# The chunk stores of the last head: from GpSimd's queue to SyncE's

## The chip, the cores and the metric

The kernel runs on one core of one Trainium2 chip. The metric is device microseconds of that core for one execution, the median of several executions. A run of a program on one core carries the state "fast" unless it lies over 1.5% above the fastest of the same kernel.

Engine names: PE is TensorE, DVE VectorE, ACT ScalarE, POOL GpSimd, SP SyncE. A "DMA engine" is one of the 16 that move bytes for this core; it is another thing than the engine that *issues* a transfer.

## The reference

Attention for one query per head, with its gradients: 64 heads (2 x 32), 8192 keys of 128 numbers, bf16.

```python
def _fwd_reference(q, k, v):
    scale = q.shape[-1] ** -0.5
    scores = jnp.einsum("bhqd,bhkd->bhqk", q, k) * scale
    p = _softmax(scores, axis=-1)
    return jnp.einsum("bhqk,bhkd->bhqd", p, v)

def reference(q, k, v, grad_out):          # shortened
    _out, _vjp = jax.vjp(_fwd_reference, q, k, v)
    return (_out, *_vjp(grad_out))          # out, dq, dk, dv
```

k and v are read once and dk and dv written once, 134 MB each: 537 MB in all, 2 MB for one head and one tensor.

## The kernel before

Every head has a tile of k and a tile of v, 128 partitions x 64 x 128 numbers (2 MB, 16 KB a partition). SyncE issues the loads, GpSimd the stores. VectorE writes dv and dk into the same tiles, in four chunks of 16 x 128 numbers a partition, and the tile is stored when its last chunk is made. Only the last head is stored chunk by chunk (4 KB a partition, 512 KB a chunk).

```python
SPREAD = range(5, 64, 9)              # heads 5, 14, 23, 32, 41, 50, 59
...
    load_eng = nc.sync
    store_eng = nc.gpsimd
    pin = tc.keep_in_program_order
...
    def by_rows(eng, dst, src, rows):
        p = 0
        for m in rows:
            pin(eng.dma_start(out=dst[p : p + m], in_=src[p : p + m], max_dma_last_dim=NT * D))
            p += m
...
    def outer(i, w, c, ends):         # one chunk of dv (w = 1) or dk (w = 0) of head i
        ...                           # VectorE writes the chunk into h.tile[w]
        if c + 1 in ends:
            at = ends.index(c + 1)
            b0, b1 = (ends[at - 1] if at else 0) * CH, (c + 1) * CH
            dst = (dv_v if w else dk_v)[i]
            if w == 0 and i in SPREAD:
                by_rows(store_eng, dst, h.tile[w], (P - 2, 2))
            else:
                pin(store_eng.dma_start(out=dst[:, b0:b1, :], in_=h.tile[w][:, b0:b1, :]))
...
    whole = [NCH]                     # NCH = 4
    last = list(range(1, NCH + 1))
...
            outer(x[0], 1, x[1], last if x[0] == BH - 1 else whole)
...
            outer(x[0], 0, x[1], last if x[0] == BH - 1 else whole)
```

The dk of the seven heads in SPREAD goes out as two stores, of 126 and of 2 rows (the *split stores*). At the very end SyncE stores two small tiles, out and dq (16 KB each).

## Time and profile before

| | before |
|---|---|
| time, median of 3 runs at the outset | 1289.55 us (1287.81 to 1290.55) |
| span of the profiled execution | 1290.8 us |
| busy: PE, ACT, DVE | 87%, 76%, 73% |
| DMA | 9 tenths or more in 39 of 40 slices |

The page of the kernel before, its DMA lines: the busy share in tenths in 40 slices of the span, what they moved, the two queues (q0 is that of GpSimd's stores, q1 that of SyncE), and the issue group of the chunk stores with the median time from issue to landing.

```profile
DMA  9999999999999999999999999999999999999994
GB/s 390 423 427 428 427 427 426 428 427 427 427 427 428 428 426 425 412 429 426 428 426 427 427 426 428 428 426 424 426 427 428 426 421 424 427 429 426 421 383 185
...
q0 software_dynamic: 20784, 268.45, 49.4%
q1 hardware_dynamic: 19020, 268.51, 48.8%
...
out_dram<-kvt POOLq DMA_DIRECT2D x8, 512.0 KB, 22.2
```

About 427 GB/s from the second slice to the last but two: the bytes bound this kernel. Only the tail is not full. Here it is in windows of 10 us (the kernel before; after the busy times come PE's granted clock, the DMA share and GB/s):

```profile
core 0: us, PE busy (x) PEld busy (x) DVE busy (x) ACT busy (x) POOL busy (x), PEclk, DMA share, GB/s
1240.00:1250.00 10.00, 7.72 (x103) 4.84 (x101) 8.50 (x24) 4.16 (x5) 0.86 (x2) 0.93 0.87 347
1250.00:1260.00 10.00, 4.64 (x19) 1.82 (x18) 9.82 (x16) 0.00 (x0) 1.79 (x4) 0.50 0.88 366
1260.00:1270.00 10.00, 0.90 (x3) 0.63 (x3) 1.19 (x5) 0.00 (x0) 1.06 (x2) 0.50 0.66 272
1270.00:1280.00 10.00, 0.00 (x0) 0.00 (x0) 0.00 (x0) 0.00 (x0) 1.06 (x2) 0.50 0.54 220
1280.00:1290.00 10.00, 0.00 (x0) 0.00 (x0) 0.00 (x0) 0.00 (x0) 0.00 (x0) 0.50 0.18 71
```

From 1262 us on nothing computes, and a third to four fifths of the DMA capacity lies idle. Why? The timeline of GpSimd, the kernel before, has the last whole store and then the eight chunks; in brackets the idle time before each and what ended it:

```profile
start us, us, engine line op out<-in xcount [idle before <-releaser]
1246.36 0.53 POOL L411 DMA_DIRECT2D out_dram<-kvt  x1 [10.33 <-DVE ld L253]
1249.67 0.53 POOL L411 DMA_DIRECT2D out_dram<-kvt  x1 [2.77 <-DVE dS_pad L325]
1251.06 0.53 POOL L411 DMA_DIRECT2D out_dram<-kvt  x1 [0.86 <-DVE dqT L379]
1254.56 0.53 POOL L411 DMA_DIRECT2D out_dram<-kvt  x1 [2.97 <-DVE sel L362]
1259.42 0.53 POOL L411 DMA_DIRECT2D out_dram<-kvt  x1 [4.33 <-DVE kvt L394]
1264.27 0.53 POOL L411 DMA_DIRECT2D out_dram<-kvt  x1 [4.31 <-issue]
1269.18 0.53 POOL L411 DMA_DIRECT2D out_dram<-kvt  x1 [4.39 <-DMA out_dram<-kvt]
1274.13 0.53 POOL L411 DMA_DIRECT2D out_dram<-kvt  x1 [4.42 <-DMA out_dram<-kvt]
1278.99 0.53 POOL L411 DMA_DIRECT2D out_dram<-kvt  x1 [4.32 <-DMA out_dram<-kvt]
```

VectorE has made the last chunk by about 1259.3; GpSimd issues its store at 1278.99. It looks like a store queue that is fed too late.

The trace's packet records tell another story. They carry no name of a DMA engine, but one DMA engine works packet after packet with next to no gap, so its row of packets can be followed back from the last packet. For the kernel before (start us, ns, queue, bytes; the records of 4 bytes are the signals that a share of a store has landed):

```
1278.079   9 q0 4        end of the laggard's share of the last 2 MB store
1278.085 159 q0 4096     first packet of chunk 1
1278.240 159 q0 4096
...                      64 packets of 4 KB, 155 ns from start to start
1287.910 159 q0 4096     last packet of chunk 8
1288.065   9 q0 4
```

This one DMA engine, the laggard, has no gap from 1248.79 to 1288.07. Its shares of six 2 MB stores (eight packets of 16 KB, 607 ns from start to start) end at 1253.64, 1258.51, 1263.37, 1268.27, 1273.22 and 1278.08, and each of GpSimd's last six issues follows such an end by about 0.9 us. GpSimd waits *for the laggard*, with eight stores outstanding; the laggard never waits for GpSimd.

### The profile page before, as it was taken

Reading aid. Unit: us, or ns where it says so; the run is one execution under the profiler, and the core shown is the slowest. Engines: PE = TensorE matmul, PEld = TensorE weight load, DVE = VectorE, ACT = ScalarE, POOL = GpSimd, SP = SyncE. Lnnn points to the kernel's source line nnn. Section 1 sums busy time; section 2 is a strip of 40 time slices with the busy share of each in tenths; the row PEclk is TensorE's granted clock in tenths of the full one; section 3 lists DMA queues with packets and bytes.
Section 4 is the critical chain, followed back from the end, with each engine's and each line's share of the span. In section 5 each row is a group of like instructions: output and inputs, shape, how many; then the busy total and the mean of one; then the engine's idle time right before and its main releaser. Section 6 shows DMA issues by size and latency. Waiting matters only on the chain.

```text
span 1290.8 us, 42577 instructions
## 1 busy us (share of the span) xinstructions
PE 1126.7 (87%) x19268; PEld 856.4 (66%) x19268; DVE 936.1 (73%) x2122; ACT 975.1 (76%) x641; POOL 79.3 (6%) x150
## 2 busy tenths in 40 slices
PE   6999999988998988989888889899898888988870
PEld 5777777666676766766666667677666666766650
DVE  2888888777787777767667777677677776777780
ACT  6888888777787777777778777778687777877740
POOL 0000000000000000000000000000000000000000
PEclk9999999999999999989999998899899999999985
DMA  9999999999999999999999999999999999999994
GB/s 390 423 427 428 427 427 426 428 427 427 427 427 428 428 426 425 412 429 426 428 426 427 427 426 428 428 426 424 426 427 428 426 421 424 427 429 426 421 383 185
DMA packets 39985, 539.67 MB, mean 418 GB/s; under 512 B 5116, under 2 KB 5116, under 8 KB 6396
## 3 DMA queue, kind: packets, MB, share of 16 engines
q0 software_dynamic: 20784, 268.45, 49.4%
q1 hardware_dynamic: 19020, 268.51, 48.8%
q8 instruction: 150, 2.46, 0.7%
q14 instruction: 31, 0.25, 0.0%
HBM read 268.47 MB, written 268.47 MB: 416 GB/s over the span
## 4 chain that ended last, share of the span: by engine, by line
DMA 37%; another core or an unknown queue 27%; PE 20%; DVE 7%; issue 5%; ACT 1%; SPq 1%; POOL 0%; POOLq 0%; ACTq 0%
DMA kvt<-in_v_dram 17%; DMA kvt<-in_k_dram 13%; PE tp L184 9%; DMA out_dram<-kvt 6%; PE acc L339 5%; DVE kvt L394 4%; PE dpw L195 3%; PE sw L195 2%; DVE sel L362 1%; ACT ev L186 1%; SPq L98 1%; PE dpw L282 1%; DMA qd_nat<-in_q_dram 1%; DVE sel L356 0%
## 5 line engine op out<-in xcount | busy, mean ns | idle before, releaser
L186 ACT COPY ev<-tp 128x2048 bf16<-128x2048 bf16 x512 | 954.3, 1865 | 269.2 <-PE tp L184 257.6
L184 PE MATMUL tp<-ident_bf,kvt 128*128 128x128 bf16 x8192 | 556.0, 222 | 99.2 <-DMA kvt<-in_v_dram 75.4
L394 DVE TENSOR_TENSOR kvt<-qb,pair 128x2048 bf16<-128x2048 bf16 x512 | 621.4, 1214 | 0.3
L184 PEld LDWEIGHTS <-kvt 128*128 128x128 bf16 x8192 | 486.4, 100 | 106.7 <-DMA kvt<-in_v_dram 79.1
L195 PEld LDWEIGHTS <-ev 128*128 128x128 bf16 x8192 | 243.1, 96 | 208.1 <-issue 150.5
L339 PE MATMUL acc<-kvt,dS_pad 128*64 128x512 bf16 x1024 | 167.3, 409 | 1.6 <-DVE dqT L379 1.6
L339 PE MATMUL acc<-kvt,E_pad 128*64 128x512 bf16 x1024 | 160.5, 394 | 0.0
L195 PE MATMUL dpw<-qdT,ev 128*128 128x1 bf16 x4096 | 140.8, 164 | 17.6 <-DVE qb L177 16.6
L362 DVE SCALAR_TENSOR_TENSOR sel<-acc,diag,sel 128x128 f32<-128x128 f32 x384 | 134.7, 351 | 13.6
L195 PE MATMUL sw<-qdT,ev 128*128 128x1 bf16 x4096 | 141.8, 164 | 1.1 <-ACT ev L186 1.1
L411 POOL DMA_DIRECT2D out_dram<-kvt x127 | 68.0, 535 | 1121.0 <-DVE kvt L394 950.5
L207 DVE TENSOR_REDUCE mp<-sw 128x1 f32<-128x64 f32 x64 | 14.4, 224 | 149.7 <-PE sw L195 149.7
L339 PEld LDWEIGHTS <-dS_pad 128*64 128x64 bf16 x1024 | 37.6, 111 | 25.1 <-issue 5.1
L247 DVE CAST E_pad<-E_f 128x64 bf16<-128x64 f32 x64 | 12.5, 195 | 55.5 <-ACT E_f L238 55.5
L339 PEld LDWEIGHTS <-E_pad 128*64 128x64 bf16 x1024 | 36.3, 108 | 21.1 <-issue 0.4
L253 DVE CUSTOM_DVE_ANT_0 junk<-E_f,dpw 128x64 bf16<-128x64 f32 x64 | 14.1, 221 | 48.9 <-PE dpw L195 48.9
L376 PE MATMUL acc<-ones,sel 128*128 128x1 f32 x256 | 43.4, 239 | 6.2 <-DVE sel L362 6.2
L282 PE MATMUL dpw<-ld,ones 128*128 128x1 f32 x256 | 46.3, 250 | 0.1
L356 DVE TENSOR_SCALAR sel<-acc,diag 128x128 f32<-128x128 f32 x128 | 44.1, 344 | 0.0
L376 PEld LDWEIGHTS acc<-ones,sel 128*128 128x128 f32 x256 | 39.1, 193 | 7.3 <-DVE sel L362 7.3
L177 DVE CAST qb<-dpw 128x128 bf16<-128x128 f32 x128 | 35.5, 277 | 6.0 <-PE dpw L168 6.0
L282 PEld LDWEIGHTS dpw<-ld,ones 128*128 128x128 f32 x256 | 38.2, 189 | 0.5 <-DVE ld L253 0.5
(44 smaller groups left out, 313.3 us busy)
## 6 DMA issues: line engine op xcount, KB each, us to landing
out_dram<-kvt POOLq DMA_DIRECT2D x119, 2048.0 KB, 67.1
kvt<-in_v_dram SPq DMA_DIRECT2D x64, 2048.0 KB, 20.9
kvt<-in_k_dram SPq DMA_DIRECT2D x63, 2048.0 KB, 21.1
out_dram<-kvt POOLq DMA_DIRECT2D x7, 2016.0 KB, 70.6
out_dram<-kvt POOLq DMA_DIRECT2D x8, 512.0 KB, 22.2
kvt<-in_k_dram SPq DMA_DIRECT2D x2, 512.0 KB, 4.4
kvt<-in_k_dram SPq DMA_DIRECT2D x1, 1024.0 KB, 7.0
out_dram<-kvt POOLq DMA_DIRECT2D x7, 32.0 KB, 70.6
```

Source lines behind the costliest of these rows:

```text
L177: pin(nc.vector.tensor_copy(out=h.qb[w][:], in_=h.qbp))
L184: pin(nc.tensor.transpose(tp[:, t, :], src[:, c * CH + t, :], ident_bf[:]))
L186: pin(nc.scalar.copy(out=ev[:], in_=tp[:]))
L195: nc.tensor.matmul(dst[:, c * CH + t : c * CH + t + 1], lhsT=ev[:, t, :], rhs=qdT[:, w, i : i + 1], start=True, stop=True,)
L207: pin(nc.vector.reduce_max(out=h.mp[:], in_=h.s, axis=AX.X))
L282: nc.tensor.matmul(out, lhsT=ones[:].to_broadcast([P, P]), rhs=col, start=True, stop=True)
L339: nc.tensor.matmul(h.acc[w][g : g + CW, :], lhsT=wts[:, n0 : n0 + CW], rhs=rows[:, n0 : n0 + QT, :].rearrange("p n d -> p (n d)"), start=( ...
L356: nc.vector.tensor_scalar(out=h.sel[:], in0=block, scalar1=diag[:, 0:1], scalar2=None, op0=ALU.mult)
L362: nc.vector.scalar_tensor_tensor(out=h.sel[:], in0=block, scalar=diag[:, b : b + 1], in1=h.sel[:], op0=ALU.mult, op1=ALU.add,)
L376: nc.tensor.matmul(h.acc[w][:, 0:1], lhsT=h.sel[:], rhs=ones[:], start=True, stop=True)
L394: nc.vector.tensor_tensor(out=h.tile[w][:, n0 : n0 + CH, :].rearrange("p n (e t) -> p n e t", t=2), in0=h.qb[w][:] .rearrange("p (e t) -> ...
L411: pin(store_eng.dma_start(out=dst[:, b0:b1, :], in_=h.tile[w][:, b0:b1, :]))
```

## The change

The intent: the eight chunk stores no longer queue behind GpSimd's waits. SyncE, which has nothing to issue after its last load, issues them as soon as the chunks are made.

```diff
             if w == 0 and i in SPREAD:
                 by_rows(store_eng, dst, h.tile[w], (P - 2, 2))
             else:
-                pin(store_eng.dma_start(out=dst[:, b0:b1, :], in_=h.tile[w][:, b0:b1, :]))
+                eng = load_eng if len(ends) > 1 else store_eng
+                pin(eng.dma_start(out=dst[:, b0:b1, :], in_=h.tile[w][:, b0:b1, :]))
```

## The prediction

> **What bounds the kernel now.** DMA: the page's 40 slices show it 9 tenths busy or more in 39, at about 427 GB/s; PE (87%), ACT (76%) and DVE (73%) are below. So only the tail, where the eight chunk stores are, can change. Windows of the tail show the DMA share falling: 0.87 (1240-1250 us), 0.88, 0.66, 0.54, 0.16 (1280-1291). Stores seem late: in the timeline GpSimd issues the eight at 1249.67, 1251.06, 1254.56, 1259.42, 1264.27, 1269.18, 1274.13 and 1278.99, although VectorE made the last chunk by about 1259.3. Waits of 4.3-4.4 us between them are for landings of earlier stores.
>
> **But those waits are not the critical path.** The trace's packet records name no DMA engine, but packets of one engine follow each other almost without a gap. Followed back from the last packet (end 1288.07), one DMA engine, the laggard, is busy without a gap from 1248.79: six groups of eight 16 KB packets (611 ns each; its shares of 2 MB stores), ending at 1253.64, 1258.51, 1263.37, 1268.27, 1273.22, 1278.08, then 64 packets of 4 KB (155 ns apart), its shares of all eight chunks. GpSimd's issues follow those group ends by about 0.9 us: it is held by the laggard's backlog (eight stores outstanding), so the laggard never starves. The DMA engines that idle (1265-1280) are those ahead of it; they finish at 1281.4-1281.8.
>
> **What the change does.**
> - Takes eight issues (0.53 us each) and waits of 4.4 us from GpSimd; adds eight issues (about 0.33 us each, as the loads') to SyncE, which has nothing to issue between 1215.5 and 1262. The chunks should go at 1249 to 1259.5: the last some 19 us earlier.
> - Bytes and shares per DMA engine stay: 128 partitions, 4 KB each. The Trainium skill ("DMA: Bandwidth & Descriptors", "Issuing engines are not separate DMA queues") says that DMAs of all issuers run on the same 16 DMA engines; here loads and stores share the 427 GB/s, which agrees. Its "Queues, rings and completion order": a DMA engine round-robins its queues by packet. So on the laggard 4 KB chunk packets will alternate with 16 KB packets of the backlog: first chunks land early, the last 2 MB store later (about 1285, not 1278), and the sum, 48 x 0.607 + 64 x 0.155 = 39.1 us from 1248.8, is the same: end about 1288.
> - The other DMA engines finish up to 15 us earlier; nothing waits for them.
> - 1288.07 to the end at 1290.8 stays. The small stores (16 KB) are now queued behind the chunks: 256 B packets of 18 ns, nothing.
>
> About 0 of the 19 us is critical.
>
> **Predicted:** 1289.3 us, 1286.0 to 1292.0 (8 in 10). Faster by over 2%: 2%; within 2%: 97%; slower: 1%.
>
> **What the profile would show.** Right: chunk issues move to SyncE and end by about 1260; GpSimd's waits of 4.4 us are gone; the DMA share rises in 1255-1265, then falls to about one engine of 16 (0.06) before 1288; the last packets end near 1288 in one gapless chain. Wrong: that chain ends before 1286, or has gaps.
>
> **What would make it wrong.** The hardware queue splits these stores otherwise, so that the laggard gets less (its 10 us of chunks, 0.8%, is the most to win); the laggard is slow because of the software queue itself; alternating two queues costs time; or the small stores wait for a chunk's landing, end last and add 1-2 us.

## The result and the profile after

| | before | after |
|---|---|---|
| median, 4 runs each | 1290.05 us (1287.81 to 1291.21) | 1287.83 us (1286.27 to 1289.27) |
| ratio | | 0.9985, 95% interval 0.9965 to 1.0004: the same |
| span of the profiled execution | 1290.8 us | 1286.9 us |
| last chunk issued | 1278.99 | by 1257.78 |
| last packet to the end of the span | 2.74 us | 2.05 us |

A ratio here is the mean time of one kernel's fast runs over that of the other's in the same rounds, so not quite the ratio of the medians quoted beside it.

The page of the kernel after, the same lines:

```profile
DMA  9999999999999999999999999999999999999995
GB/s 388 424 425 427 427 427 427 426 427 428 428 426 427 428 427 426 416 429 427 427 427 429 427 427 427 427 424 424 426 427 428 426 427 424 427 428 428 424 392 216
...
q1 hardware_dynamic: 20172, 272.70, 49.8%
q0 software_dynamic: 19632, 264.25, 48.7%
...
out_dram<-kvt SPq DMA_DIRECT2D x8, 512.0 KB, 24.0
```

4.2 MB went from q0 to q1, and a chunk takes no less time from issue to landing than before (median 24.0 us, before 22.2). The timeline of SyncE's queue after, then that of GpSimd:

```profile
start us, us, engine line op out<-in xcount [idle before <-releaser]
1245.80 11.98 SPq L412 DMA_DIRECT2D out_dram<-kvt  x8
1259.23 4.90 SPq L489 DMA_DIRECT2D out_dram<-nat  x2
```

```profile
1243.38 0.53 POOL L412 DMA_DIRECT2D out_dram<-kvt  x1 [9.19 <-DVE ld L253]
```

All eight chunks are issued within 12 us, and GpSimd's last store is issued by 1243.9. The windows of the tail after:

```profile
core 0: us, PE busy (x) PEld busy (x) DVE busy (x) ACT busy (x) POOL busy (x), PEclk, DMA share, GB/s
1240.00:1250.00 10.00, 7.76 (x68) 3.73 (x66) 9.31 (x20) 1.86 (x1) 0.53 (x1) 0.70 0.92 376
1250.00:1260.00 10.00, 3.62 (x14) 1.82 (x14) 8.03 (x17) 0.00 (x0) 0.00 (x0) 0.50 1.00 411
1260.00:1270.00 10.00, 0.00 (x0) 0.00 (x0) 0.00 (x0) 0.00 (x0) 0.00 (x0) 0.50 0.61 255
1270.00:1280.00 10.00, 0.00 (x0) 0.00 (x0) 0.00 (x0) 0.00 (x0) 0.00 (x0) 0.50 0.48 202
1280.00:1290.00 10.00, 0.00 (x0) 0.00 (x0) 0.00 (x0) 0.00 (x0) 0.00 (x0) 0.55 0.06 22
```

The DMA share is higher until 1260 and lower from there on: the DMA engines that are ahead finish sooner, and the laggard still works alone at the end (one of 16 is 0.06). Its row of packets after, in two places (in the first, the records of several DMA engines fit together with the row's end; each row that fits alternates like this):

```
1251.654 159 q1 4096     chunks and whole stores in turn
1251.809 611 q0 16384
1252.416 159 q1 4096
1252.571 611 q0 16384
...
1284.402 159 q1 4096
1284.557 159 q1 4096     last packet of chunk 8
1284.713   9 q1 4
1284.718  18 q1 256      the small stores, eight packets
...
1284.837   9 q1 4        last record
```

The two queues alternate packet by packet, without a gap: the chunks begin early and the whole stores end late. The last 2 MB store landed 12.4 us before the end of the span in before and 5.4 us in after.

**How much of the 3.9 us between the two profiled spans belongs to the change?** The lead is there before the change can act: the last load is issued at 1215.21 in before and at 1213.08 in after. Each store signals 16 landings, one for each DMA engine. I call *lag* the time from the 15th to the last of these, read at the 126-row store of head 59, which lands at 1244 to 1252 us, when no chunk is stored yet. The lag is 6.51 us in before and 3.27 us in after; the 15th landing comes at the same time in both (1242.62 and 1242.61). So the lag accounts for 3.24 us, and the last packet indeed ends 3.23 us earlier (1288.07 and 1284.85). The other 0.69 us of the 3.9 are the time from the last packet to the end, 2.74 against 2.05 us; they come up again below.

### The profile page after: what moved, and what is told of

Same layout as the page of the kernel before. It is cut to its first block, busy times and chain, and to the rows that moved or that the text cites. A ratio compares the mean times of both kernels' runs of the same rounds, so it can differ in the third digit from the quotient of the medians.

```text
span 1286.9 us, 42575 instructions
## 1 busy us (share of the span) xinstructions
PE 1131.8 (88%) x19268; PEld 860.1 (67%) x19268; DVE 935.9 (73%) x2122; ACT 975.2 (76%) x641; POOL 75.1 (6%) x142
## 4 chain that ended last, share of the span: by engine, by line
DMA 38%; PE 26%; another core or an unknown queue 19%; DVE 10%; issue 4%; ACT 1%; SPq 1%; POOL 0%; POOLq 0%; DVEq 0%; ACTq 0%
DMA kvt<-in_v_dram 29%; PE tp L184 11%; PE acc L339 6%; DVE kvt L394 6%; DMA kvt<-in_k_dram 5%; DMA out_dram<-kvt 4%; PE dpw L195 3%; PE sw L195 3%; DVE sel L362 2%; ACT ev L186 1%; PE dpw L282 1%; SPq L98 1%; DVE sel L356 1%; DMA qd_nat<-in_q_dram 1%
## 5 line engine op out<-in xcount | busy, mean ns | idle before, releaser
L412 POOL DMA_DIRECT2D out_dram<-kvt x119 | 63.7, 536 | 1087.6 <-DVE kvt L394 922.1
```

The costliest lines, as they stand in the source:

```text
L412: pin(eng.dma_start(out=dst[:, b0:b1, :], in_=h.tile[w][:, b0:b1, :]))
```

## The experiments

Two theories. **L (laggard):** the end is set by the bytes that one DMA engine still has; when the chunks are issued doesn't matter while it has a backlog. **I (issue):** the tail is bound by late issues, and what the change gained was lost again elsewhere. Times are in the table at the end of this section.

### The change again

No edit.

> The changed kernel again, in more rounds, to have its size beside the other runs. Theory L (laggard: one DMA engine has a gapless backlog that holds all its shares of the eight chunks, so the end is its bytes and not the time of issue): ratio to before 0.998 to 1.000. Theory I (issue: the DMA share falls in the tail because GpSimd issues late, so issuing 19 us earlier must pay): below 0.995.

Measured: ratio 0.9979 (0.9951 to 1.0007), 1287.2 us. An issue some 21 us earlier isn't worth 0.5%. The profiled execution had a lag of 0.3 us and a span of 1285.0 us.

### The last head whole, from GpSimd

```diff
-            outer(x[0], 1, x[1], last if x[0] == BH - 1 else whole)
+            outer(x[0], 1, x[1], whole)
...
-            outer(x[0], 0, x[1], last if x[0] == BH - 1 else whole)
+            outer(x[0], 0, x[1], whole)
```

> The last head stored whole by GpSimd, two stores of 2 MB in place of eight chunks. A chunk's packets then can't start before the whole tile is made. Theory L: the laggard reaches these bytes only about 29 us after the end of its earlier backlog began to be drained, long after the tile is made; 16 packets of 16 KB (9.7 us) in place of 64 of 4 KB (9.9 us); the time is that of before within 1 us (ratio 0.999 to 1.001). Theory I: the first bytes of each tile are offered 3.6 us later than when chunked, 3 to 4 us slower (ratio about 1.003).

Measured: ratio 0.9997 (0.9965 to 1.0029), correct. The interval doesn't exclude theory I's 1.003 by itself; the timeline of GpSimd in this kernel says more:

```profile
1244.52 0.53 POOL L411 DMA_DIRECT2D out_dram<-kvt  x1 [9.82 <-DVE ld L253]
1251.61 0.53 POOL L411 DMA_DIRECT2D out_dram<-kvt  x1 [6.56 <-DVE sel L356]
1257.69 0.53 POOL L411 DMA_DIRECT2D out_dram<-kvt  x1 [5.55 <-DVE sel L356]
```

With two stores in place of eight GpSimd meets no limit of eight outstanding stores and issues its last one at 1257.69, 21 us earlier than before, from the same queue. The time is that of before, within 0.4%. This run alone changes two things, the time of issue and the size of the stores, which could cancel; beside the run before it, in which the early issue alone was worth nothing measurable, the cutting into chunks isn't worth anything measurable either.

### Without the dk chunks, from GpSimd and from SyncE

Both are wrong on purpose: dk of the last head isn't stored (the check of the result found it missing and the other outputs right).

```diff
-                pin(store_eng.dma_start(out=dst[:, b0:b1, :], in_=h.tile[w][:, b0:b1, :]))
+                if not (len(ends) > 1 and w == 0):
+                    pin(store_eng.dma_start(out=dst[:, b0:b1, :], in_=h.tile[w][:, b0:b1, :]))
```

(the second kernel has the same condition around the changed line, with `eng`).

> Wrong on purpose: the kernel before without the last four chunk stores (dK of the last head is not stored). Theory L: the laggard has 32 packets of 155 ns less: 5.0 us faster (ratio about 0.996). Theory I: the last issue is then the fourth, at 1259.4 in place of 1279.0, and the end follows it: 15 to 20 us faster (ratio 0.985 to 0.988).

> Wrong on purpose: the changed kernel without the last four chunk stores. Theory L: 5.0 us faster than the changed kernel, as in the kernel before (ratio to before about 0.995 to 0.996). Theory I: the issues were early already, so the loss of the last four, at 1252 to 1256, moves the end by their spread of issue, 4 to 6 us; this run alone doesn't tell the two apart, only beside the run before it (theory L: both lose the same; theory I: 15 to 20 against 4 to 6 us).

Measured, from GpSimd: ratio 0.9959 (0.9923 to 0.9995), which is 5.3 us of 1290, with an interval from 0.6 to 9.9 us (the six runs scatter from 1281.29 to 1291.20 us; their mean, 1285.67, is 4.3 us below that of the eleven runs of before). From SyncE: 0.9939 (0.9911 to 0.9966), mean 1282.13 against 1287.38 us of the changed kernel: 5.25 us (six runs each, and all six faster than the fastest of the changed kernel). Theory L asked for 5.0 us (32 packets of 155 ns) in both; theory I for 15 to 20 us with GpSimd. With GpSimd even the end of the interval, 9.9 us, is far from theory I's 15. That both come so near to 5.0 is luck with GpSimd, where the interval is wide. This is the clearest verdict against theory I: the last issue moved from 1279 to 1262.3 us,

```profile
1262.31 0.53 POOL L412 DMA_DIRECT2D out_dram<-kvt  x1 [4.29 <-DMA out_dram<-kvt]
```

and the time followed the bytes, not the issue. The size alone doesn't say that they are the *laggard's* bytes: the store takes a sixteenth from each DMA engine, and 2 MB at 427 GB/s are 4.9 us too. That one DMA engine sets the end is read from its gapless row while the DMA share falls to 0.18 and below, and from the lags that follow.

### The kernel before again: the lag

No edit.

> The kernel before itself, as a measure of the scatter and for another look at its laggard. In the six profiles so far the last DMA engine's lag behind the 15th, taken at the landings of head 59's split store (before any chunk is stored), is 6.5, 5.0 and 8.0 us with the chunks on GpSimd and 3.3, 0.3 and 0.0 us with them on SyncE, and the span is about 1285 us plus that lag (plus 5.0 where dK was left out). Theory L: this execution's span is 1285 plus its own lag, within 1.5 us; ratio to before 0.999 to 1.001. If the lag is luck of the execution, it may be small here; if the changed program causes it, it is 5 us or more here.

Measured: ratio 1.0005 (0.998 to 1.003), lag 2.3 us, span 1288.1 us (0.8 us over 1285 plus the lag). The lag is below 5 us here, so chunks on GpSimd don't force a large one. All executions profiled with seven split stores, except the one with rows 0 to 119 and 120 to 127 apart (below):

| execution | lag us | span us | span minus lag | last packet to end |
|---|---|---|---|---|
| before | 6.5 | 1290.8 | 1284.3 | 2.74 |
| before again | 2.3 | 1288.1 | 1285.8 | 2.74 |
| whole from GpSimd | 5.0 | 1288.9 | 1283.9 | 2.49 |
| before without dk (5.0 added to the span) | 8.0 | 1293.5 | 1285.5 | 2.56 |
| after | 3.3 | 1286.9 | 1283.6 | 2.05 |
| after again | 0.3 | 1285.0 | 1284.7 | 2.05 |
| after, third look | 4.7 | 1288.5 | 1283.8 | 2.05 |
| after without dk (5.0 added) | 0.0 | 1284.9 | 1284.9 | 2.35 |

The span runs over 8.6 us and the span minus the lag over 2.2: most of the scatter between executions is the laggard's lag, which is there before the first chunk is stored. That is theory L from another side, as a correlation over eight executions.

### Luck or program?

With the change the first lags were smaller, and no time had been over 1289.3 us.

> The changed kernel a third time, for the open question whether its program keeps the laggard's lag small or whether that was luck. Nine profiles so far, lag at head 59's split store: chunks on GpSimd 6.5, 5.0, 8.0, 2.3 us; on SyncE 3.3, 0.3, 0.0 and 7.4 us (the last in the run with rows 0 to 119 and 120 to 127 apart). If it is luck: all six times scatter over 1286 to 1295 us as those of before do, and the lag may be anything in 0 to 8 us. If the program does it: all six within 1286 to 1289.5 us, lag under 3.5 us, ratio to before 0.996 to 0.999.

Measured: ratio 0.9998 (0.9976 to 1.002); times from 1286.94 to 1292.71 us; lag 4.7 us. All three bounds that "the program does it" had set (times, lag and ratio) are broken, so the lag is, by all that is seen, luck of the execution. A small leaning of the program isn't excluded by these few looks.

### Less for the laggard to do, and the size of the change in quiet runs

In before, around 1241 to 1249 us, one DMA engine's share of head 59's 126-row store is 8 KB packets of about 641 ns, where most 8 KB packets take 309 ns; why was not found. It has 18 of them, which are 9 rows, where a whole store gives it 8. (An estimate from this: 14 DMA engines with 9 rows each make up the 126, so a split store spares two DMA engines most of their share.) The edit leaves this store whole, on SyncE's and on GpSimd's variant:

```diff
-SPREAD = range(5, 64, 9)
+SPREAD = range(5, 59, 9)
```

> The changed kernel with head 59's dK stored as one DMA in place of 126 and 2 rows. In the profile of before the laggard took 18 packets of 8 KB in this store at about 641 ns each, 11.5 us, where an unsplit store takes it 8 x 0.607 = 4.9 us. Theory L: what the laggard has less to do moves the end, until the next DMA engine is last: 3 to 6 us faster than the changed kernel (ratio to before 0.993 to 0.996), more than the change itself. Rival (the end isn't set by one DMA engine's bytes): no change against the changed kernel.

> The kernel before (chunks on GpSimd) with the same edit. Theory L: the same 3 to 6 us faster than before (ratio 0.995 to 0.998), and within 1 us of the run before it when both have the same lag, although GpSimd issues its last chunk late again. Theory I: no gain without the early issue.

Measured: 1283.92 us (ratio 0.9953, 0.9934 to 0.9973) with the change and 1284.63 us (0.9958, 0.9939 to 0.9977) without it, both correct. Storing head 59's dk whole is worth more than the whole change, with either issuer, and no byte was taken away, so the bytes in all aren't what sets the end. And theory I's "no gain without the early issue" is wrong: with GpSimd the last chunk was again issued late,

```profile
1271.78 0.53 POOL L411 DMA_DIRECT2D out_dram<-kvt  x1 [4.62 <-DMA out_dram<-kvt]
```

The scatter went too: six runs each within 1.3 and 0.9 us. In this quiet pair the change can be sized: means 1284.08 and 1284.71 us, 0.63 us apart (with six runs each, give or take some 0.5 us). And the trace shows where such an amount comes from. From the last packet to the end of the span the pair takes 2.02 and 2.69 us, as all kernels with eight chunks in the table take 2.05 with SyncE and 2.74 with GpSimd. The instruction records of before and after (start us, duration, engine):

```
before   1278.97  11.06  GpSimd  DRAIN      ends 1290.03, 1.95 us after the last packet
before   1288.98   0.01  SyncE   DRAIN      SyncE is ready and waits for GpSimd
before   1290.07         GpSimd  the closing barrier begins
after    1286.12   0.01  SyncE   DRAIN
after    1286.16         GpSimd  the closing barrier begins at once
```

(DRAIN is an instruction near the end of an engine's queue, which lasted here until 1.8 to 2.0 us after the last packet of the stores that this engine had issued.) With the chunks on its queue, GpSimd's draining at the end outlasts SyncE's waits for the landings by 1.1 us. After the change GpSimd's DRAIN ends at 1282.74, 2.1 us before the last packet, and SyncE's own waits, which end somewhat later, set the end. Net: 0.7 us.

### Taking the chunks from one DMA engine

```diff
+                if len(ends) > 1:
+                    for p0, p1 in ((0, 120), (120, P)):
+                        pin(eng.dma_start(out=dst[p0:p1, b0:b1, :], in_=h.tile[w][p0:p1, b0:b1, :]))
+                else:
+                    pin(eng.dma_start(out=dst[:, b0:b1, :], in_=h.tile[w][:, b0:b1, :]))
```

> The changed kernel with each chunk store of the last head cut into rows 0 to 119 and 120 to 127. By the Trainium skill's rule for the number of DMA engines of a store the first goes to 15 of them and the second to the lowest 8, so one DMA engine gets no chunk bytes and eight get 9 rows in place of 8. Theory L: faster by up to the lag (0 to 6 us) if the laggard is the relieved one; slower by about 1.2 us (8 packets of 155 ns) if it is one of the eight; else the same as the changed kernel. Theory I: the same or slower, by the extra issues alone.

Measured: 1295.12 us, ratio 1.0041 (1.0017 to 1.0064), 8.55 us over the changed kernel's mean of its own rounds (1295.93 against 1287.38 us). It was run at another time. None of theory L's three outcomes; theory I had asked for "the same or slower". The rule stands in the Trainium skill's page "DMA: Bandwidth & Descriptors", section "Why a DMA increments its semaphore by 16 and not by 1". The number of landings is as it has it: 8 x 15 + 8 x 8 for the chunks and 2 x 16 for the small stores are 216 signals on SyncE's queue, and the trace has 216. Which DMA engines they come from, no trace shows. But after 1250 us 37 of 298 packets of 16 KB took over 900 ns, where in the changed kernel it was 1 of 288. So packets were slow in this execution, and the experiment doesn't tell which DMA engine is the laggard. It has a second flaw: with sixteen stores in place of eight SyncE waited for landings too (15.4 us in four waits), and the last chunk was issued at 1284.3 and the small stores at 1287.1 and 1288.0, against 1256.3 and by 1264.1 with the change. Packets of whole stores went on until 1292.4, so late issues needn't be what cost the time, but this run doesn't part the two. Its lag at head 59, 7.4 us, was large as well, with the chunks on SyncE.

### Fewer split stores, and none

`SPREAD = range(5, 50, 9)`, and `SPREAD = range(0)`, both on the changed kernel.

> The changed kernel with the split stores of heads 50 and 59 left whole (five split stores in place of seven). Theory L: the one of head 59 gave 3.4 us against the changed kernel because the laggard does it at half rate and late. The one of head 50 lies 190 us before the end and its lag may be evened out or not: between 2 us faster and 3 us slower than with head 59 alone left whole (ratio to before 0.993 to 0.998).

> The changed kernel with no split store at all. If the split stores make the scatter (slow packets, lag of the last DMA engine), the times lie within 1.5 us of each other; whether they are faster or slower than with the splits is open: the splits relieve two DMA engines of 7 rows each time, so if those two are slower than the rest by nature, they are the laggards now, and the time is 1290 us or more; if not, 1284 us or less.

Measured: with five split stores 1284.84 us (0.997, 0.9951 to 0.9989), between the bounds and no better than with six. With none 1304.13 us (1.0118, 1.0097 to 1.0139), four runs within 0.5 us. Both halves of the expectation hold: without split stores the scatter is gone, and one DMA engine is far behind: at the store that lands last at 1235 us the last of 16 signals comes 22.8 us after the 15th. One signal is late and not two, as the expectation had in mind, and the gap to the 15th grows steadily: 1.9 us at 171 us, 12.7 at 658 and 22.1 at 1144. The splits are needed; their price is the scatter, and the last one comes too late to pay.

| kernel | median us | ratio to before (95%) |
|---|---|---|
| after, again | 1287.20 | 0.9979 (0.9951 to 1.0007) |
| whole from GpSimd | 1289.13 | 0.9997 (0.9965 to 1.0029) |
| before without dk (wrong) | 1284.42 | 0.9959 (0.9923 to 0.9995) |
| after without dk (wrong) | 1282.02 | 0.9939 (0.9911 to 0.9966) |
| before, again | 1289.97 | 1.0005 (0.998 to 1.003) |
| after, split stores to head 50 | 1283.92 | 0.9953 (0.9934 to 0.9973) |
| before, split stores to head 50 | 1284.63 | 0.9958 (0.9939 to 0.9977) |
| after, rows 120 and 8 | 1295.12 | 1.0041 (1.0017 to 1.0064) |
| after, third look | 1287.96 | 0.9998 (0.9976 to 1.002) |
| after, split stores to head 41 | 1284.84 | 0.997 (0.9951 to 0.9989) |
| after, no split store | 1304.13 | 1.0118 (1.0097 to 1.0139) |

The kernel before: 1289.95, 1289.77 and 1288.67 us (11 runs each). The best version is the changed kernel with head 59 stored whole: 1283.92 us, faster than both kernels, by less than 0.5%.

## Why the prediction was right or wrong

- **"Those waits are not the critical path": right, and shown.** Issuing 21 us earlier, from SyncE or by whole stores from GpSimd, left the time within noise; taking 5.0 us of bytes from the laggard took 5.3 us from the time with GpSimd (0.6 to 9.9) and 5.25 us with SyncE.
- **The time: right.** 1287.83 us lies in 1286.0 to 1292.0, within 2% as given 97%. The forecast was 0.3 us less than 1289.55; the three looks at the change give ratios of 0.9985, 0.9979 and 0.9998.
- **The sign of being wrong, "that chain ends before 1286": it came.** The last packet ended at 1284.85, in a gapless chain. This sign was badly chosen: it took the lag of one execution (6.5 us) as fixed, and the profiled execution of the kernel after had 3.3 us; the difference is the whole of the 3.23 us. With a lag of 4.7 us, in the third look, the last packet of the same kernel ended at 1286.42.
- **The queues alternate by packet, and the 2 MB stores end later: right.** The forecast put the last 2 MB store about 5.8 us before the end of the span (1285 of 1290.8); it was 5.4 us.
- **"1288.07 to the end at 1290.8 stays": wrong in size.** This term went from 2.74 to 2.05 us. GpSimd's drain was on the critical path at the very end, and the prediction hadn't looked at it. The quiet pair gives 0.63 us in time for it. This is the change's own effect; the rest of the 2.2 us between the first medians is within the scatter, of which most, as far as the profiled executions show, is the laggard's lag; it is there before the chunks are stored.
- **SyncE's issues: mis-sized, harmlessly.** Estimated at 0.33 us each from the loads; the eight took 0.34 to 1.72 us, median 1.05. Why they take longer than the loads was not tested. They fit in the time in which the chunks are made.
- **The small stores "wait for a chunk's landing": it happened, without cost.** SyncE waited 3.9 us for a store's landing between the two small stores; both were issued by 1264.1, 20 us before the laggard came to them, and their packets add 0.13 us to its row.
- **"The DMA share rises in 1255-1265, then falls to about 0.06 before 1288": right in kind.** 1.00 in place of 0.88 in 1250-1260, but already below before in 1260-1270 (0.61 against 0.66, in an execution that was 3 us ahead); 0.06 in the last window.

Open: which of the 16 DMA engines the laggard is, why one falls behind by 23 us when no store is split, and what sets its lag in an execution.

## What to carry to other kernels

When an issuing engine waits for landings while DMA capacity is idle, ask which of the 16 DMA engines it waits for: if one of them has a gapless row of packets to the end, as here, its bytes are the time, and issuing earlier from another queue only reorders them. Test such a tail by taking bytes away, not by moving issues: the time should fall by about the time of the packets taken. And look at what closes the kernel: an engine that still has to drain its own stores can hold the end after the last packet.

## What the Trainium skill lacked or had wrong

- "DMA: Bandwidth & Descriptors", section "Issuing engines are not separate DMA queues", says that issuing from several engines "will only save the time on the sequencer it takes to initiate the DMA". The runs agree for the transfers (ratios 0.9979 to 0.9998) and add one thing it lacks: GpSimd's drain at the end of the kernel, 2.74 against 2.05 us from the last packet to the end.
- The same page, "Queues, rings and completion order", has round-robin by packet. The trace agrees and shows what that means when packet sizes differ: a 4 KB packet (155 ns) for each 16 KB packet (607 ns), so the shares are by packet and not by bytes. It calls some 9 to 17 descriptors a typical packet; where the row can be followed without doubt (1276.7 to 1279.7 us), the turn changed after every single record of 4 or 16 KB.
- The same page, "Specifications", gives about 27 GiB/s for one DMA engine. 16,384 bytes in 607 ns are 27.0 GB/s: the number holds with GB in place of GiB.
- The same page, "Latency and other measured facts", says that DMA engines 7 and 15 are usually slower than the others in traces, with a cause that it calls a guess. It lacks how far this carries within one kernel: without split stores one DMA engine was 23 us behind the 15th late in the kernel, with them 0 to 8 us, and the last one set the end. Whether it is one of those two, these traces can't say, as they don't name the DMA engines.
- The page's rule for the number of DMA engines of a store ("Why a DMA increments its semaphore by 16 and not by 1") held: 216 signals counted. It lacks what such shapes can cost: in the one execution with them, 37 of 298 packets of 16 KB took over 900 ns, against 1 of 288.
